# Three moves in the order of work: the product of gate sums on GpSimd, the search for gates on VectorE, one gate line on TensorE

## The chip, the cores and the metric

One Trainium2 chip, of which the kernel uses one core. The metric is the device time of one execution in microseconds, less is better. The engines are named as in the profile: PE is TensorE's matrix multiplication and PEld its weight loads, DVE is VectorE, ACT is ScalarE, POOL is GpSimd, SP is the engine that issues most DMAs.

## The reference

The computation is attention with pooled queries, followed by a layer that sends 128 of 576 tokens of each batch through a small network. All arrays are float32. B is 8, H is 8, S is 1152, D is 64.

```python
# attention
q_pool = q.reshape(B, H, S // 2, 2, D).mean(axis=3)
scores = np.matmul(q_pool, k.transpose(0, 1, 3, 2)) / np.sqrt(D)
attn = softmax(scores)                         # 576 x 1152 for each of 64 heads
x = heads_side_by_side(np.matmul(attn, v))     # (8, 576, 512)
# routing: 128 of 576 tokens in each batch
scores = np.einsum('bsd,d->bs', x, w_gate)
out = x.copy()
for b in range(B):
    top_idx = np.argpartition(-scores[b], 128)[:128]
    xe = x[b, top_idx]
    ye = np.maximum(xe @ w1, 0.0) @ w2         # 512 -> 1024 -> 512
    g = 1.0 / (1.0 + np.exp(-scores[b, top_idx]))
    out[b, top_idx] = x[b, top_idx] + g[:, None] * ye
```

## The kernel before

**Halves.** The work runs over 32 pairs of heads (8 batches, 4 pairs each), and each pair in two halves of 288 pooled queries, so 64 halves in all. The order of instructions on each engine is written out by hand; each engine takes its queue in that order and waits by semaphores. In the loop of `run` half number h issues, in this order: the scores of h (PE, L818, 36 matmuls in nine tiles of `ps`; after each tile ACT takes the exponent into `p`, L825); the places called "mid"; `gated` of half h-3; `folded` of h; the places called "sums"; `multiplied` of h-2; the values of h-1 (PE, L836, 36 matmuls, copied by ACT into `two`, L844, and added on POOL into `av`, L846); and at last the places called "end". The PSUM tile `ps` has four buffers, so a fifth tile waits until ACT has emptied the first.

**Around the exponents.** `folded` lets POOL add exponents (`acc`, L857, three additions in a half), and DVE add them up further (`fold`, L862; `sum`, L872). `drained` transposes `av` into `avb` (DVE, L915). `multiplied` multiplies `avb` with the weights of the gate (`prod`, POOL, L925). `gated` sums that up on DVE (`red`, L981), and in the second half of a pair it multiplies the sum with the reciprocal of the softmax's sums into `part` (L986: on POOL, and on DVE for the last two pairs of the last batch).

**Routing.** With the fourth pair of a batch the generator `routed` starts. It is cut into pieces by `yield`, and the value yielded says at which place of a half the next piece runs. Its steps: `line` (DVE, L1010) adds the four `part`. In batches 0 to 5 ACT copies it into 32 partitions and DVE adds the groups; in batch 6, the last but one, one matmul with `merge` does that (PE, L1024), and ACT copies its result into `total` (L1031). SP writes `total` to DRAM and reads it back spread over the partitions (`row`, `sc_row`, `gate_sc`, L1035 to L1038). DVE then ranks the tokens by comparisons (L1085 to L1104), and the ranks and gates go through DRAM into `lines`. Two searches over `lines` on DVE (both L1169, 128x640) find the token of each slot (`found_token`, from which `index` comes, L1178) and its gate (`own_gate`). POOL gathers the tokens with an indirect DMA (`xe`, L1188); PE transposes them (L1205), multiplies with `w1` (L1216) and `w2` (L1229); ACT multiplies with `own_gate` into `y` (L1248), POOL adds, and an indirect DMA scatters the result (L1254).

**The end.** After the last half `run` places the remaining pieces by hand: products with `w2` of batch 5 and 6 fill PE while the gate of the last batch is worked out in a chain over POOL, DVE, PE and ACT (`prod`, `red`, `part`, `line`, `diag`, L1046, and a matmul of it, L1056).

Of the kernel before, what the change touches and what calls it, by code (L numbers as in the profile page):

```python
# [10 lines left out]
P = 128  # L11
# [3 lines left out]
F32 = mybir.dt.float32  # L15
# [6 lines left out]
def _rows_of(ap_1d: bass.AP, parts: int) -> bass.AP:  # L22

    return dataclasses.replace(ap_1d, ap=[[0, parts]] + [list(x) for x in ap_1d.ap])
# [3 lines left out]
def _any_scores(  # L28
# [451 lines left out]
    in_pair = [(j, t) for j in range(2) for t in range(NF)] + [(0, NF)]  # L480
    upcoming = load_pair(*pairs[0])
    run(prepare_pair(upcoming))
    preparing = iter(())
    routing = iter(())
# [43 lines left out]
    for _ in range(2):  # L528
        advance(None)
        one, two = None, one  # L530
    run(routing)
    run(routed(B - 1, x))


class _Plain:
# [439 lines left out]
    def gated(self, half):  # L975

        nc, pair, hb = self.nc, half["pair"], self.HB
        if half["s"] == 0:
            pair["red"] = self.small.tile([P, self.QB], F32, name="red")
        ns = slice(half["s"] * hb, (half["s"] + 1) * hb)  # L980
        nc.vector.tensor_reduce(pair["red"][:, ns], pair["prod"][:, ns, :], AX.X, ALU.add)  # L981
        if half["s"] == 1:

            ending = pair["b"] == self.B - 1 and pair["hp"] >= self.NPAIR - 2
            engine = nc.vector if ending else nc.gpsimd
            engine.tensor_tensor(  # L986
                out=pair["part"][:, pair["hp"], :],
                in0=pair["red"][:, :],
                in1=pair["rec"][:, :],
                op=ALU.mult,  # L990
            )
            if pair["hp"] == self.NPAIR - 1:
                self.routing.append([pair["b"], self.routed(pair["b"], pair["part"]), "sums"])
# [6 lines left out]
    def routed(self, b, part):  # L1000


        nc, ffn, Sp, NT, NF = self.nc, self.ffn, self.Sp, self.NT, self.NF
        tiles = [(t, P if t < NF else self.TAIL) for t in range(NT)]
        mid = "mid" if b < self.B - 2 else True
# [7 lines left out]
        sc = ffn.tile([P, NT], F32, name="gate_sc")  # L1013
        if b < self.B - 1:

            yield "mid"
            if b < self.B - 2:
                groups = self.side_by_side(line)
                yield True
                total = self.added(groups)  # L1020
            else:
                total = self.small.tile([BLK, self.QB], F32, name="total")
                ps = self.banks()[:, 0, 0 : self.QB]
                nc.tensor.matmul(  # L1024
                    ps,
                    lhsT=self.merge.rearrange("p g j -> p (g j)"),
                    rhs=line[:, :],
                    start=True,
                    stop=True,
                )  # L1030
                nc.scalar.copy(total[:, :], ps[0:BLK, :])  # L1031
            sc_row = ffn.tile([P, NT * P], F32, name="sc_row")
            row = self.dram.tile([Sp], F32, name="row")
            nc.gpsimd.memset(sc[:, NF:], 0.0)
            nc.sync.dma_start(row.rearrange("(i n) -> i n", i=BLK), total[:, :])  # L1035
            nc.sync.dma_start(sc_row[:, 0:Sp], _rows_of(row[:], P))
            nc.sync.dma_start(sc[:, 0:NF], row[0 : NF * P].rearrange("(t p) -> p t", p=P))
            nc.sync.dma_start(  # L1038
                sc[0 : self.TAIL, NF:], row[NF * P :].rearrange("(t p) -> p t", p=self.TAIL)
            )  # L1040
            yield True
            yield True
        else:

            diag = ffn.tile([P, self.QB, BLK], F32, name="diag", bufs=1)
            nc.vector.tensor_tensor(  # L1046
                out=diag[:, :, :],
                in0=line[:, :].unsqueeze(2).broadcast_to([P, self.QB, BLK]),
                in1=self.same[:, :].unsqueeze(1).broadcast_to([P, self.QB, BLK]),
                op=ALU.mult,  # L1050
            )
            yield True
            sc_row = self.line_of_scores()
            ps = self.banks()
            for s in range(2):
                nc.tensor.matmul(  # L1056
                    ps[:, s, 0 : self.HALF],
                    lhsT=self.ones[:, :],
                    rhs=diag[:, s * self.HB : (s + 1) * self.HB, :].rearrange("p n i -> p (n i)"),
                    start=True,  # L1060
                    stop=True,
                )
            nc.scalar.copy(
                sc_row[:, 0:Sp].rearrange("p (i s n) -> p s n i", s=2, n=self.HB),
                ps[:, :, 0 : self.HALF].rearrange("p s (n i) -> p s n i", i=BLK),
            )
            yield True
            self.columns(sc, sc_row)
# [3 lines left out]
            out=gate[:, :], in0=sc[:, :], scalar1=-88.0, scalar2=None, op0=ALU.max  # L1072
# [7 lines left out]
        for t, rows in tiles:  # L1080
            at = t * P
            cmp = ffn.tile([P, Sp], F32, name="cmp", bufs=1)
            own = sc[0:rows, t : t + 1]
            if t > 0:
                nc.vector.tensor_scalar(  # L1085
                    out=cmp[0:rows, 0:at],
# [8 lines left out]
                out=cmp[0:rows, at:Sp],  # L1095
# [9 lines left out]
                out=tie[0:rows, 0:rows],  # L1105
# [16 lines left out]
            out=gate[:, :], in0=gate[:, :], scalar1=1.0, scalar2=None, op0=ALU.add  # L1122
# [5 lines left out]
        else:  # L1128
# [8 lines left out]
            lines = ffn.tile([P, P, 2, NT], F32, name="lines", bufs=1)  # L1137
            nc.sync.dma_start(lines.rearrange("p i a t -> p (i a t)"), _rows_of(row[:], P))

        for s0, w in self.slots:  # L1140
            pick = ffn.tile([P, NT, P], F32, name="pick", bufs=1)
            index = ffn.tile([P, 1], I32, name="index")
            own_gate = ffn.tile([P, 1], F32, name="own_gate")
            if b == self.B - 1:

                nc.vector.tensor_tensor(
                    out=pick[:, :, 0:w],
                    in0=self.slot_f[:, s0 : s0 + w].unsqueeze(1).broadcast_to([P, NT, w]),
                    in1=rank[:, :].unsqueeze(2).broadcast_to([P, NT, w]),
                    op=ALU.is_equal,  # L1150
                )
                yield True
                ps = self.banks()[:, 0, 0:2]
                for t, rows in tiles:
                    nc.tensor.matmul(  # L1155
                        ps[0:w, :],
                        lhsT=pick[0:rows, t, 0:w],
                        rhs=meta[0:rows, t, :],
                        start=(t == 0),
                        stop=(t == NT - 1),  # L1160
                    )
                nc.scalar.copy(index[0:w, :], ps[0:w, 0:1])
                nc.scalar.copy(own_gate[0:w, :], ps[0:w, 1:2])
            else:
                yield True

                found = self.small.tile([P, 1], F32, name="found_token")
                for of, to in ((self.token_line, found), (lines[:, :, 1, :], own_gate)):
                    nc.vector.scalar_tensor_tensor(  # L1169
                        out=pick.rearrange("p t i -> p (t i)").rearrange("p (i t) -> p i t", t=NT)[0:w],  # L1170
                        in0=lines[0:w, :, 0, :],
                        scalar=self.token[0:w, s0 // P : s0 // P + 1],
                        in1=of[0:w, :, :],
                        op0=ALU.is_equal,
                        op1=ALU.mult,
                        accum_out=to[0:w, :],
                    )
                nc.vector.tensor_scalar(  # L1178
                    out=index[0:w, :],
                    in0=found[0:w, :],  # L1180
                    scalar1=float(b * Sp),
                    scalar2=None,
                    op0=ALU.add,
                )

                yield "sums" if b < self.B - 2 else True
            xe = ffn.tile([P, self.Dm], F32, name="xe")
            nc.gpsimd.indirect_dma_start(  # L1188
                out=xe[0:w, :],
# [5 lines left out]
            )  # L1195
            yield True
            if b < self.B - 2:
                yield True
            if b != self.B - 2:
                yield mid  # L1200
# [36 lines left out]
            if b == self.B - 1:  # L1237
                nc.vector.scalar_tensor_tensor(
                    out=xe[0:w, :],
# [6 lines left out]
            else:  # L1246
# [8 lines left out]
                out=rows_out,  # L1255
# [65 lines left out]
    def run(self):  # L1321
        nc = self.nc
        pairs = [(b, hp) for b in range(self.B) for hp in range(self.NPAIR)]
        n_halves = 2 * len(pairs)
        halves = []
# [10 lines left out]
        for h in range(n_halves):  # L1336
            n, s = divmod(h, 2)
            if s == 0:
                pair = upcoming
# [12 lines left out]
            half = {"pair": pair, "s": s}  # L1352
            halves.append(half)
            self.scores(half)
            if h > 1:

                of = halves[h - 2 - s]["pair"]
# [5 lines left out]
            if h > 2:  # L1363
                self.gated(halves[h - 3])
            self.folded(half)
            self.units("sums")
            if h > 1:
                self.multiplied(halves[h - 2])
# [18 lines left out]
        def pieces(unit, n=None):  # L1387
            for i, _ in enumerate(unit):
                if i + 1 == n:
                    break  # L1390
# [8 lines left out]
        self.drained(halves[-1])  # L1399
        self.multiplied(halves[-2])  # L1400
        self.multiplied(halves[-1])
        self.gated(halves[-2])
        pieces(older, 1)
        self.normalized(halves[-1]["pair"])
        for half in (halves[-3], halves[-1]):
            self.divided(half["pair"])
            self.stored(half["pair"])
        self.gated(halves[-1])
        _, new, _ = self.routing.pop()

        pieces(new, 1)
# [76 lines left out]
```

## Time and profile before

| what | us |
|---|---|
| median of 4 runs | 703.91 (703.86 to 703.99) |
| the profiled execution's own time | 703.96 |
| its span, from the first to the last instruction | 702.2 |
| PE busy | 692.0 (99%) |
| PE weight loads busy | 515.1 (73%) |
| DVE busy | 478.6 (68%) |
| ACT busy | 445.4 (63%) |
| POOL busy | 491.7 (70%) |
| granted TensorE clock | 0.998 |

The profiled execution lies 0.05 us above the median; 1.76 us of its time lie outside the span. Busy time is what an engine's instructions cover; matmuls are pipelined, so their rows overlap a little, and a row's start tells more than its length. In the chain of waits each row starts where the row before it ends, so that its lengths add up to time on the path to the end; "x72" there counts 36 matmuls that are each made of two passes.

### The profile page before, as it was taken

To read this page: it belongs to the slowest core of one execution; us is meant where nothing else is said; L and a number is where in the kernel's file an instruction comes from. 1 tells how busy PE (TensorE), PEld (TensorE's weight loads), DVE (VectorE), ACT (ScalarE), POOL (GpSimd) and SP (SyncE) were. 2 spreads that over 40 slices of the span, in tenths; PEclk is the share of its full clock that TensorE was granted. 3 is DMA by queue.
4 is the path that set the end of the run, shared out by engine and by line. 5 is a ranking of instruction groups with operands and counts; after the bars stand their busy time and mean duration, and the time that the engine had idled before them with its cause. 6 is when DMAs were issued, how large, how long until landed. Compare 5 with 4: busy or idle time off the path is not lost.

```text
span 702.2 us, 23365 instructions
## 1 busy us (share of the span) xinstructions
PE 692.0 (99%) x9948; PEld 515.1 (73%) x9948; DVE 478.6 (68%) x770; ACT 445.4 (63%) x963; POOL 491.7 (70%) x475
## 2 busy tenths in 40 slices
PE   8999999999999999999999999999999999999996
PEld 6667899999756887568775787757877578676673
DVE  3866677788836887278863888548884588668740
ACT  6677778777647775477745777557775477747210
POOL 5788888779837796397954879548886479956620
PEclk9999999999999999999999999999999999999999
DMA  8888886858782396824956269652686528711300
GB/s 178 174 183 178 182 155 130 141 120 155 131 146 68 78 162 117 153 67 95 183 98 122 68 125 169 118 90 64 139 154 131 89 53 174 135 19 47 59 33 35
DMA packets 389490, 82.86 MB, mean 118 GB/s; under 512 B 376640, under 2 KB 376640, under 8 KB 389376
## 3 DMA queue, kind: packets, MB, share of 16 engines
q1 hardware_dynamic: 387872, 76.49, 57.3%
q0 software_dynamic: 1280, 4.20, 1.8%
q8 instruction: 80, 1.31, 0.8%
q10 hardware_dynamic: 224, 0.59, 0.3%
q14 instruction: 34, 0.28, 0.1%
HBM read 69.65 MB, written 11.59 MB: 116 GB/s over the span
## 4 chain that ended last, share of the span: by engine, by line
PE 96%; ACT 1%; DMA 1%; DVE 1%; POOL 0%; SPq 0%; issue 0%; POOLq 0%; DVEq 0%; ACTq 0%
PE ps L836 40%; PE ps L818 39%; PE ps L1216 8%; PE ps L1229 7%; DMA kb<-in_k_dram 1%; ACT p L825 1%; PE ps L1205 1%; SPq L759 0%; POOL prod L925 0%; DVE diag L1046 0%; PE ps L1155 0%; PE ps L1056 0%; ACT two L844 0%; PE ps L783 0%; POOL av L846 0%
## 5 line engine op out<-in xcount | busy, mean ns | idle before, releaser
L825 ACT ACTIVATE p<-ps 128x576 f32<-128x576 f32 x576 | 320.0, 697 | 1.0 <-PE ps L818 1.0
L836 PE MATMUL ps<-p,v_sb 64*64 64x288 f32 x4608 | 294.0, 403 | 0.0
L818 PE MATMUL ps<-qT,kT 64*64 64x288 f32 x4608 | 293.3, 403 | 0.0
L857 POOL TENSOR_TENSOR acc<-p 128x576 f32<-128x576 f32 x192 | 274.1, 1456 | 7.8 <-ACT p L825 7.7
L836 PEld LDWEIGHTS ps<-p,v_sb 64*64 64x64 f32 x4608 | 211.3, 133 | 69.5 <-ACT p L825 9.0
L818 PEld LDWEIGHTS ps<-qT,kT 64*64 64x64 f32 x4608 | 210.4, 133 | 69.2 <-ACT p L825 6.9
L862 DVE TRANSPOSE_TENSOR_REDUCE fold<-p 128x54 f32<-128x1728 f32 x64 | 126.0, 1969 | 56.9 <-ACT p L825 56.9
L862 DVE TRANSPOSE_TENSOR_REDUCE fold<-acc 128x54 f32<-128x1728 f32 x64 | 125.2, 1956 | 57.7 <-POOL acc L857 57.6
L844 ACT COPY two<-ps 128x576 f32<-128x576 f32 x64 | 40.9, 639 | 151.6 <-PE ps L836 148.2
L846 POOL TENSOR_TENSOR av<-two 128x288 f32<-128x288 f32 x64 | 51.2, 801 | 92.9 <-ACT two L844 82.5
L915 DVE STREAM_TRANSPOSE avb<-av 128x288 f32<-128x288 f32 x64 | 29.1, 454 | 67.2 <-POOL av L846 66.7
L1216 PEld LDWEIGHTS ps<-xeT,w 128*128 128x128 f32 x512 | 57.8, 192 | 2.7 <-ACT p L825 2.6
L1216 PE MATMUL ps<-xeT,w 128*128 128x128 f32 x512 | 59.3, 277 | 0.0
L1229 PE MATMUL ps<-w,hT 128*128 128x512 f32 x128 | 57.5, 599 | 0.0
L986 POOL TENSOR_TENSOR part<-red,rec 128x18 f32<-128x18 f32 x30 | 6.8, 226 | 64.3 <-DVE red L981 56.5
L925 POOL TENSOR_TENSOR prod<-avb,w_gate 128x288 f32<-128x288 f32 x64 | 51.6, 806 | 0.2
L732 POOL TENSOR_TENSOR qp<-qb 128x576 f32<-128x576 f32 x31 | 43.8, 1413 | 2.2 <-DMA qb<-in_q_dram 2.2
L1229 PEld LDWEIGHTS ps<-w,hT 128*128 128x128 f32 x128 | 23.5, 190 | 28.1 <-issue 25.8
L735 DVE STREAM_TRANSPOSE kT<-kb 128x1152 f32<-128x1152 f32 x31 | 42.0, 1355 | 0.0
L902 ACT ACTIVATE sums<-total,tiny 32x18 f32<-32x18 f32 x124 | 38.2, 308 | 2.9 <-DVE total L893 1.1
L959 POOL TENSOR_TENSOR x<-avb,rec 128x576 f32<-128x576 f32 x32 | 37.1, 1160 | 0.0
L1224 ACT ACTIVATE hT<-ps 128x512 f32<-128x512 f32 x16 | 9.6, 597 | 39.1 <-PE ps L1216 39.1
(96 smaller groups left out, 312.3 us busy)
## 6 DMA issues: line engine op xcount, KB each, us to landing
kb<-in_k_dram SPq DMA_DIRECT2D x124, 144.0 KB
qb<-in_q_dram SPq DMA_DIRECT2D x124, 144.0 KB
v_sb<-in_v_dram SPq DMA_DIRECT2D x124, 144.0 KB
out_dram<-x SPq DMA_DIRECT2D x128, 72.0 KB
lines<-row_rank SPq DMA_DIRECT2D x7, 640.0 KB
w<-in_moe_w_dram SPq DMA_DIRECT2D x8, 512.0 KB
sc_row<-row SPq DMA_DIRECT2D x7, 288.0 KB
acc<-in_q_dram ACTq DMA_DIRECT2D x2, 288.0 KB
```

The lines of the kernel that those rows point to most:

```text
L732: nc.gpsimd.tensor_tensor(out=qp[:, :, :], in0=pair["q"][:, :, 0, :], in1=pair["q"][:, :, 1, :], op=ALU.add)
L735: nc.vector.transpose(kT.rearrange("p (c g i) -> p c g i", c=self.NC, i=BLK), pair["k"].rearrange("p (g c) d -> p c g d", c=self.NC),)
L818: nc.tensor.matmul(sc[keys, j, 0:n], lhsT=pair["kT"][rows, c * P + keys.start : c * P + keys.stop], rhs=pair["qT"][rows, qs], start=True, ...
L825: nc.scalar.activation(p[:, c // G, c % G, :, :], sc[:, :, 0:n], AF.Exp, scale=self.scale)
L836: nc.tensor.matmul(av[j * self.D : (j + 1) * self.D, e, 0:n], lhsT=half["pair"]["v"][keys, j, c, :], rhs=half["p"][keys, c // G, c % G, j, :],
L844: nc.scalar.copy(two[:, :, :], av[:, :, 0:n])
L846: nc.gpsimd.tensor_tensor(out=half["av"][:, :], in0=two[:, 0, :], in1=two[:, 1, :], op=ALU.add)
L857: nc.gpsimd.tensor_tensor(out=acc[:, u, :], in0=units[:, 0, u, :], in1=units[:, 1, u, :], op=ALU.add)
L862: nc.vector.tensor_reduce(fold[:, a, :], of.rearrange("p u (m d) -> p (u m) d", d=BLK), AX.X, ALU.add, apply_transpose=True,)
L925: self.nc.gpsimd.tensor_tensor(out=pair["prod"][:, ns, :], in0=pair["avb"][:, ns, :], in1=self.w_gate[:, hp : hp + 1, :].broadcast_to([P, ...
L1216: nc.tensor.matmul(pv[:, f, 0:w], lhsT=self.w1[:, c, (f0 + f) * P : (f0 + f + 1) * P], rhs=xeT[:, c, 0:w], start=(c == 0), stop=(c == self ...
L1229: nc.tensor.matmul(ps[0:w, 0 : self.Dm], lhsT=hT[:, f, 0:w], rhs=self.w2[:, f, :], start=(f == 0), stop=(f == self.NFC - 1),)
```

## The change

Three moves. No instruction is added or removed, and none changes its size.

1. `gated` is split. The product into `part` becomes a function `scored` of its own, and `run` calls it behind `folded`, so that POOL has `part` behind the three additions of exponents and not ahead of them, in all 30 products on POOL. At the end the DVE product of the last pair but one stands behind the last transpose into `avb`, where it stood ahead of it.
2. In batches 0 to 5 the search for `own_gate` runs in the "end" of the half after the one in which the token is searched; `index` follows the first search at once. In batch 6 both stay in the same half, and `index` is computed between them.
3. In batch 6 the matmul of the gate line (L1024) and the copy into `total` move from the "mid" of a half to its "end": on PE from ahead of the transposes of batch 5 (L1205) and the values (L836) to behind them, ahead of the next scores; on ACT from ahead of the copies of L1208 and L844 to behind them, ahead of the next nine exponents. A `yield` further on is left out in this batch, so that the comparisons keep their half.

The order of SP's queue stays as it was. The cut diff:

```diff
@@ def gated
         nc.vector.tensor_reduce(pair["red"][:, ns], pair["prod"][:, ns, :], AX.X, ALU.add)
+
+    def scored(self, half):
+        nc, pair = self.nc, half["pair"]
         if half["s"] == 1:
             ending = pair["b"] == self.B - 1 and pair["hp"] >= self.NPAIR - 2
             engine = nc.vector if ending else nc.gpsimd
...
@@ def routed
-            yield "mid"
+            yield mid
             if b < self.B - 2:
                 groups = self.side_by_side(line)
                 yield True
                 total = self.added(groups)
             else:
+                yield True
                 total = self.small.tile([BLK, self.QB], F32, name="total")
...
             yield True
-            yield True
+            if b < self.B - 2:
+                yield True
...
-                found = self.small.tile([P, 1], F32, name="found_token")
-                for of, to in ((self.token_line, found), (lines[:, :, 1, :], own_gate)):
+                def search(of, to):
+                    at = ffn.tile([P, NT, P], F32, name="pick", bufs=1)
                     nc.vector.scalar_tensor_tensor(
...
+                found = self.small.tile([P, 1], F32, name="found_token")
+                search(self.token_line, found)
                 nc.vector.tensor_scalar(
...
+                if b == self.B - 2:
+                    search(lines[:, :, 1, :], own_gate)
                 yield "sums" if b < self.B - 2 else True
...
             if b < self.B - 2:
+                search(lines[:, :, 1, :], own_gate)
                 yield True
@@ def run
             if h > 2:
                 self.gated(halves[h - 3])
             self.folded(half)
+            if h > 2:
+                self.scored(halves[h - 3])
             self.units("sums")
...
         self.multiplied(halves[-1])
+        self.scored(halves[-3])
         self.gated(halves[-2])
...
         self.gated(halves[-1])
+        self.scored(halves[-1])
```

More of the change, by code (lines that the diff above doesn't have):

```diff
@@ L1140, in routed @@
         for s0, w in self.slots:
-            pick = ffn.tile([P, NT, P], F32, name="pick", bufs=1)
             index = ffn.tile([P, 1], I32, name="index")
@@ L1144, in routed @@
             if b == self.B - 1:
+                pick = ffn.tile([P, NT, P], F32, name="pick", bufs=1)
                 nc.vector.tensor_tensor(
@@ L1165, in routed @@
                 yield True
-                found = self.small.tile([P, 1], F32, name="found_token")
-                for of, to in ((self.token_line, found), (lines[:, :, 1, :], own_gate)):
+                def search(of, to):
+                    at = ffn.tile([P, NT, P], F32, name="pick", bufs=1)
                     nc.vector.scalar_tensor_tensor(
-                        out=pick.rearrange("p t i -> p (t i)").rearrange("p (i t) -> p i t", t=NT)[0:w],
+                        out=at.rearrange("p t i -> p (t i)").rearrange("p (i t) -> p i t", t=NT)[0:w],
                         in0=lines[0:w, :, 0, :],
```

## Prediction

> **What bounds the kernel now.** I read the page's busy times and the chain that ended last first.
>
> ```profile
> PE 692.0 (99%) x9948; PEld 515.1 (73%) x9948; DVE 478.6 (68%) x770; ACT 445.4 (63%) x963; POOL 491.7 (70%) x475
> PE 96%; ACT 1%; DMA 1%; DVE 1%; POOL 0%; SPq 0%; issue 0%; POOLq 0%; DVEq 0%; ACTq 0%
> ```
>
> PE carries the chain. The other engines stand still for a third of the time, so an earlier step on POOL or DVE is worth something only where PE waits for it. Of the waits, POOL's largest for `part` is this one (us, times, longest):
>
> ```profile
> POOL part L986 <- DVE red L981: 56.5, 28, 4.9
> ```
>
> With its two other releasers (4.6 and 3.2 us) POOL stands 64.3 us ahead of `part`. But this is idle time of an engine that is off the chain. So I looked for places where PE itself is late. The chain in order of time (start, length, what) repeats 4.37 us for the scores and 4.37 to 4.41 us for the values of a half, nearly without exception. Here is batch 5, with nothing but the transposes between them:
>
> ```profile
> 512.43 4.37 PE ps L818 x72
> 516.80 0.59 PE ps L1205 x4
> 517.39 4.53 PE ps L836 x72
> 521.91 4.37 PE ps L818 x72
> ```
>
> and here is the same place of batch 6, where the gate line stands:
>
> ```profile
> 597.90 0.47 ACT two L844
> 598.44 5.01 ACT p L825 x9
> 603.45 0.35 PE ps L1024 x2
> 603.80 0.48 PE ps L1205 x4
> 604.28 4.53 PE ps L836 x72
> 608.80 4.37 PE ps L818 x72
> ```
>
> From the start of the scores to the start of the values it takes 517.39 - 512.43 = 4.96 us in batch 5. In batch 6 the values before end at 597.83 (593.45 + 4.38 in the same view), and it takes 604.28 - 597.83 = 6.45 us. The 1.49 us between them are the price of the gate line where it stands: 1.25 us of waiting, and the matmul. The timeline says what it waits for (start, length, engine, line):
>
> ```profile
> 603.03 0.26 DVE L1010 TENSOR_REDUCE line<-part 128x18 f32<-128x72 f32 x1
> 603.43 0.37 PE L1024 MATMUL ps<-line,merge 128*128 128x18 f32 x2 [1.25 <-ACT p L825]
> ```
>
> The row names an exponent. The ninth exponent ends only at 603.44, while the matmul's operand `line` is done at 603.29 and its first weights load at 603.40: I take `line` to be the releaser. If it is an exponent that frees a tile of `ps`, the sum stays the same, as the changed place has neither wait.
>
> **Part 3, the gate line, is the only part that I expect on the path.** Removed: 1.49 us, as L1205 then follows the scores directly as in batch 5. Added: the same matmul between values and scores. `line` is then needed at about 597.83 + 4.96 + 4.53 = 607.3 and was ready at 603.29, so no wait. The tile it takes needs the exponent two places further on than the one L1205 needs, long done by then. What remains is its own pitch and the passage between 64x64 and 128x128 tiles. Own pitch: from L1024 to L1205 it is 603.65 - 603.43 = 0.22 us; the similar matmul at the end (L938, 36 columns) is followed after 0.14 us. Passage: four transposes take 0.59 us behind scores and 0.44 us among 128x128 tiles, so 0.15 going in; values take 4.53 us behind them and 4.37 behind scores, so 0.16 coming out. Sum 0.14 to 0.22 + 0.31 = 0.45 to 0.53; I take 0.45, as the pitch of 0.22 contains some of the way in. Bounds: 0.14 with no passage at all, and 0.75 (0.59 + 0.16) if it costs as much as the transposes. Net: -1.49 + 0.45 = -1.04 us, between -1.35 and -0.74.
>
> Here a rule speaks against this part. TensorEngine Tiling (Array Packing), Key Properties, says that changing the tiling mode drains TensorE. The rows above show such a cost (0.15 and 0.16 us), and before, L1024 shared one pair of passages with L1205, while it now has its own. Without the rule the sum would be -1.49 + 0.22 = -1.27 us, with it -1.04 us.
>
> Behind L1024 in PE's queue are the next scores; on ACT the copy into `total` (0.17 us) now stands behind `two` and ahead of nine exponents, which all wait for it. That cover is in the trace: in the half at 633.8 us ACT has the gate's exponential (0.21 us) in just this place, and the chain still gives 4.37 us for scores and for values. SP's issue of `row` is at 609.23 although `total` was done at 605.07, because four stores stand ahead of it. `total` will now be done at about 608.1, so SP is hardly later; the last read is issued at 612.3, and the comparisons start at 627.4 in their unchanged half. If that cover were gone, PE would lose what the landing exceeds 627.4 by.
>
> **Part 1, `part` behind the additions.** 30 products of 0.23 us change places with 30 x 3 additions of 1.46 us. Queued behind `part` are now `prod` and `av`, ahead of them less waiting than before: `av` waits for ACT's `two` anyway (82.5 us over the run). Who waits for `part`: only `line`, once in a batch, on DVE behind a fold that waits for the same additions; it comes at most 0.23 us behind them. POOL begins the additions up to 4.9 us earlier, DVE gets its fold earlier, and PE takes no note: 0. If POOL were the bound, the 64.3 us would be the gain; the chain puts POOL at 0%.
>
> **Part 2, the search.** One search of 1.91 us (the first takes 1.12) and its readout of 0.08 move by a half, in six batches, 12 us of DVE in all; `index` comes 2.0 us earlier. The half with both is the crowded one (DVE busy 8.71 of 8.75 us at 589.08 to 597.83). `own_gate` is needed by `y`, some 45 us after (505.5 against 549.6 in batch 5). The gather stands behind the additions on POOL and is issued at 506.95 with a median of 4.2 us to landing, for transposes at 516.73: early before, no later after. On PE: 0. The cover is DVE's slack to the exponents' buffers: the fold of `acc` ends at 602.7, and its `p` is written again at 609.5, 6.8 us later, against 2.0 us moved. Without cover it would be 6 x 2.0 = 12 us.
>
> **The end.** There the chain leaves PE for 6 us, and part 1 changes DVE's order:
>
> ```profile
> 656.51 0.79 POOL L846 TENSOR_TENSOR av<-two 128x288 f32<-128x288 f32 x1 [1.15 <-ACT two L844]
> 656.72 0.61 DVE L986 TENSOR_TENSOR part<-red,rec 128x18 f32<-128x18 f32 x1
> 657.26 1.54 POOL L925 TENSOR_TENSOR prod<-avb,w_gate 128x288 f32<-128x288 f32 x2
> 657.33 0.48 DVE L915 STREAM_TRANSPOSE avb<-av 128x288 f32<-128x288 f32 x1
> 658.08 0.46 DVE L981 TENSOR_REDUCE red<-prod 128x9 f32<-128x288 f32 x1 [0.28 <-POOL prod L925]
> 658.84 0.45 DVE L981 TENSOR_REDUCE red<-prod 128x9 f32<-128x288 f32 x1
> 659.32 0.63 DVE L986 TENSOR_TENSOR part<-red,rec 128x18 f32<-128x18 f32 x1
> 660.30 1.35 DVE L1046 TENSOR_TENSOR diag<-line,same 128x576 f32<-128x576 f32 x1
> 661.80 1.21 PE L1056 MATMUL ps<-diag,ones 128*128 128x288 f32 x4
> ```
>
> The two `part` on DVE end 0.03 us behind a POOL instruction (657.33 against 657.30; 659.95 against 659.90, as the second POOL row of 1.13 us began at 658.77), 0.6 us for what POOL does in 0.23. The first moves behind L915, to about 657.8, into the first product, which ends at 658.05; the reduction that follows began at 658.08. So +0.03 us if DVE gets in between the two products as it did at 657.30. If not, it ends at 658.84, the reductions and the reciprocal follow to 659.95, the second `part` waits for the second product of L959 until 661.06, and `diag` (0.62 us once POOL is done at 661.03) ends at 662.03 where it ended at 661.65: +0.38. An earlier end gains no more than 0.1, since PE's transposes end at 661.70. I take +0.03, the row in the same place.
>
> The page SBUF — State Buffer, Who interferes with whom, makes that an exclusive lock: a DVE instruction with two inputs in SBUF and a reading GpSimd instruction exclude each other for a whole instruction, and issue order decides. It agrees with the ends of the rows, and would make +0.03 or +0.38 as the second product issues behind or ahead of DVE.
>
> **Sum.** -1.04 + 0.03 = -1.01 us on the profiled 703.96, 702.95; on the median, 0.05 lower, 702.90. Changes within 0.2% (1.41 us, about what a measurement of this kernel can tell from no change: 702.50 to 705.32) count as the same.
>
> **Rivals.** *Everything gained (0.15):* L1024 costs 0.14 without passage, and the freed POOL also takes away what the values lose in the six rows of 4.41 us (6 x 0.04 = 0.24): 703.91 - 1.49 + 0.14 - 0.24 = 702.32, faster. For it: weight loads of L836 wait 9.0 us for exponents in 43 places. Against: PE's rows hardly show it, and POOL is not what they wait for. *The end pays (0.15):* DVE loses its place between the products: 702.87 + 0.38 = 703.25, the same by the bound. *The change brings nothing (0.06):* the matmul waits in its new place for its tile as long as it did: 703.91. Against: the exponents are done 4 us before. *Slower (0.07):* POOL's additions, up to 4.9 us earlier, now run beside ACT's exponents and slow them. The ninth score tile of a half and the values' tile are already waited for by 0.2 us (35 and 43 weight loads), so PE loses as soon as nine exponents take over some 5.3 us in place of 5.00; 0.2 us in 28 halves are 5.6: 703.91 - 1.04 + 5.6 = 708.5. Against: they take 5.00 us in halves where additions run beside them (598.44 and 625.69) as in others. The forecast keeps 0.57.
>
> The range takes in the bound of the cheap matmul less the small waits (702.3, rounded up to 702.4 with the chance beyond it) and -0.74 with +0.38 (703.55): 702.4 to 703.6. Faster by over 0.2%: 0.15 and a little of the forecast's lower edge, 0.16; the same 0.77; slower 0.07.
>
> **What would show it.** Right: in batch 6 the chain goes scores, L1205 with 0.59, values 4.53, the gate matmul with 0.2 to 0.35, scores, all on PE; POOL's wait of 56.5 us for `red` is gone and stands at `av`, its busy time unchanged; L1056 starts 1.0 us earlier than before, within 0.1. Wrong: a wait on PE ahead of the gate matmul, scores of 4.6 us and more behind it, nine exponents over 5.1 us, or L1056 earlier by 0.7 us or less.

## The result, and the profile after

The changed kernel takes 704.86 us (median of 35 runs, 704.09 to 706.51), the kernel before 703.99 us beside it (55 runs, 703.6 to 705.89). The ratio is 1.0011, interval 1.0007 to 1.0016: slower by 0.8 us (the medians differ by 0.87), where 1.0 us less was predicted. By the bound of 0.2% that is no change, but it lies outside the predicted range. The profiled execution took 704.37 us, its span is 702.63 us.

Most of what the prediction listed as its proof is in the trace. First the page of the kernel after, busy times and the chain by engine:

```profile
PE 693.6 (99%) x9948; PEld 497.1 (71%) x9948; DVE 497.5 (71%) x770; ACT 446.0 (63%) x963; POOL 492.1 (70%) x475
PE 97%; DMA 1%; DVE 1%; POOL 0%; SPq 0%; issue 0%; ACT 0%; POOLq 0%; DVEq 0%; ACTq 0%
```

ACT's 1% of the chain, the wait for the gate line, is gone. PE, still the whole chain, is busy 1.6 us longer (693.6 against 692.0) with the same instructions. The waits (us, times, longest) show the first move as it was read from the code: POOL's 56.5 us for `red` have shrunk to 9.7 and stand elsewhere.

```profile
POOL av L846 <- ACT two L844: 116.9, 28, 8.8
POOL acc L857 <- ACT p L825: 36.5, 41, 1.9
PEld ps L818 <- ACT p L825: 15.3, 63, 0.4
POOL part L990 <- DVE red L981: 9.7, 10, 1.4
```

The third row was not foreseen: weight loads of the scores wait for exponents 63 times and 15.3 us, before 35 times and 6.9 us. Now the place of the gate line in batch 6, in the chain in order of time (start, length, what):

```profile
599.17 4.37 PE ps L818 x72
603.54 0.59 PE ps L1217 x4
604.12 4.53 PE ps L836 x72
608.65 0.33 PE ps L1029 x2
608.98 4.53 PE ps L818 x72
```

That is the predicted order, all on PE. From one start of scores to the next it takes 9.91 us here, 1.14 us less than before. The gate matmul costs 0.33 us of its own and 0.16 us of passage into the scores behind it (4.53 in place of 4.37). So the gain that was predicted did come. The loss stands elsewhere, in a half of the next kind (this one in batch 1):

```profile
247.44 4.67 PE ps L818 x72
252.11 4.42 PE ps L836 x72
256.53 4.37 PE ps L818 x72
```

Before, the same half took:

```profile
247.57 4.36 PE ps L818 x72
251.93 4.37 PE ps L836 x72
```

Scores of 4.67 us and values of 4.42 us stand where 4.36 and 4.37 were. There are six such halves, one in each of batches 0 to 5. By the distances from one start of scores to the next they are 0.18, 0.43, 0.41, 0.31, 0.31 and 0.34 us longer than the same halves before: 1.98 us in all. The halves around them take back 0.29 us, the end adds 0.07 us. With -1.14 us at the gate line that makes +0.62 us; from the second half's scores to the end of the span the kernel took 680.68 us, 0.64 us more than before (680.04). So the sign that the prediction hung on the whole sum failed: the first matmul of `diag` starts at 662.14 us in the chain in place of 661.81, 0.33 us later, where 1.0 us earlier was forecast.

What these six halves have in common is the gather of `xe`. Here is the timeline of the same stretch (start, length, engine, line, operation, idle time and what ended it):

```profile
247.53 0.64 ACT L844 COPY two<-ps 128x576 f32<-128x576 f32 x1 [1.91 <-POOL acc L857]
247.63 1.14 POOL L1199 DMA_INDIRECT xe<-out_dram,index  x1
248.07 0.66 ACT L825 ACTIVATE p<-ps 128x576 f32<-128x576 f32 x1
249.06 1.74 ACT L825 ACTIVATE p<-ps 128x576 f32<-128x576 f32 x3 [0.34 <-PE ps L818]
249.76 0.21 PEld L818 LDWEIGHTS ps<-qT,kT 64*64 64x64 f32 x8 [0.41 <-ACT p L825]
```

The second exponent of the half begins 0.99 us behind the first, where 0.54 us is usual, and ACT idles for 0.34 us of it, waiting for PE; 0.7 us later PE waits for an exponent, as `ps` has four buffers. But PE was not late: its matmuls still started every 0.485 us for a tile. Late is what PE reports. Here are the trace's records of PE's semaphore, which the exponents wait for, and the starts of the exponents, all counted from the start of the gather on POOL. Without a pause a report comes every 0.485 us.

```
                 gather at   reports of PE            exponents start
before, batch 1    250.84    0.14             1.38    0.02  0.55  1.08  1.61
before, batch 2    336.19    0.16  0.73       1.50    0.04  0.58  1.11  1.64
after, batch 1     247.63    0.31  1.41 1.51  1.77    0.44        1.44  1.98
after, batch 2     333.35    0.33  1.41 1.51  1.78    0.46        1.44  1.98
```

After, the second tile's report is due at 0.80 and comes at 1.41; the third's, due at 1.28, comes 0.1 us behind it; the fourth is on time. ACT would have taken the second tile at 0.98. Before, the pause is there too, and behind each gather and scatter of the loop: in this profile and the one before no report is recorded from 0.74 to 1.29 us behind their start. (Where a record is missing, as at 0.62 in batch 1 before, the exponent of 1.08 shows that the report itself had come.) But it costs nothing. The gather stands 3.5 us behind the first matmul of the scores, in the middle of these nine exponents without a gap:

```profile
248.20 5.00 ACT L825 ACTIVATE p<-ps 128x576 f32<-128x576 f32 x9
250.84 1.14 POOL L1188 DMA_INDIRECT xe<-out_dram,index  x1 [0.16 <-issue]
```

A report is due at 0.62, just ahead of the pause, and the next, due at 1.11, is wanted only at 1.61: ACT takes 0.53 us for a tile and PE 0.485 us, so ACT's distance has grown from 0.13 us at the first tile to about 0.5 us at the ninth. The change has moved the gather to 0.4 us behind the first matmul (in batch 0 to 0.4 us ahead of it). There the distance is 0.13 to 0.2 us, and a report is due in the middle of the pause.

### The profile page after: what moved, and what is told of

Its sections match the earlier page's. It is cut to its first block, busy times and chain, and to the rows that moved or that the text cites. A ratio compares the mean times of both kernels' runs of the same rounds, so it can differ in the third digit from the quotient of the medians.

```text
span 702.6 us, 23364 instructions
## 1 busy us (share of the span) xinstructions
PE 693.6 (99%) x9948; PEld 497.1 (71%) x9948; DVE 497.5 (71%) x770; ACT 446.0 (63%) x963; POOL 492.1 (70%) x475
## 3 DMA queue, kind: packets, MB, share of 16 engines
q8 instruction: 80, 1.31, 0.8%
## 4 chain that ended last, share of the span: by engine, by line
PE 97%; DMA 1%; DVE 1%; POOL 0%; SPq 0%; issue 0%; ACT 0%; POOLq 0%; DVEq 0%; ACTq 0%
PE ps L836 40%; PE ps L818 40%; PE ps L1228 8%; PE ps L1241 7%; DMA kb<-in_k_dram 1%; PE ps L1217 1%; SPq L759 0%; POOL prod L925 0%; DVE diag L1052 0%; PE ps L1161 0%; PE ps L1062 0%; PE ps L783 0%; POOL av L846 0%; DVE xe L1250 0%; POOL out_dram L1266 0%
## 5 line engine op out<-in xcount | busy, mean ns | idle before, releaser
L836 PE MATMUL ps<-p,v_sb 64*64 64x288 f32 x4608 | 293.9, 404 | 0.0
L836 PEld LDWEIGHTS ps<-p,v_sb 64*64 64x64 f32 x4608 | 204.3, 133 | 76.8 <-ACT p L825 10.5
L818 PEld LDWEIGHTS ps<-qT,kT 64*64 64x64 f32 x4608 | 199.4, 133 | 81.2 <-ACT p L825 15.3
L844 ACT COPY two<-ps 128x576 f32<-128x576 f32 x64 | 40.9, 639 | 151.3 <-PE ps L836 130.9
L1110 DVE SCALAR_TENSOR_TENSOR tie<-sc_row,gate_sc,before 128x128 f32<-128x128 f32 (+1 forms) x40 | 45.9, 1147 | 0.0
```

Of the source, the lines that this page charges most:

```text
L818: nc.tensor.matmul(sc[keys, j, 0:n], lhsT=pair["kT"][rows, c * P + keys.start : c * P + keys.stop], rhs=pair["qT"][rows, qs], start=True, ...
L836: nc.tensor.matmul(av[j * self.D : (j + 1) * self.D, e, 0:n], lhsT=half["pair"]["v"][keys, j, c, :], rhs=half["p"][keys, c // G, c % G, j, :],
L1110: nc.vector.scalar_tensor_tensor(out=tie[0:rows, 0:rows], in0=sc_row[0:rows, at : at + rows], scalar=own, in1=self.before[0:rows, 0:rows], ...
```

## The experiments

The theories, before any of these runs: the gather's pause, moved to the start of the scores (A); POOL's additions beside ACT slow the exponents (B); the moved search makes DVE late (C); the gate line costs in its new place what it saves (D). After the first group A became A2, in which the pause belongs to the execution and not to the kernel, with E beside it, in which the third move makes the loss.

The runs were made in three groups on three chips: chip 8 (the first four), chip 5 (the next four) and chip 11 (the last four), each with the kernel before beside it (704.32, 704.14 and 704.24 us). One thing must be known to read their spans: the loading at the start varies. The second half's scores began between 21.95 and 23.62 us in these profiles, without regard to the kernel, so the medians hold a scatter of up to 1.7 us that is none of the change's. The table gives the span from there to the end ("body"), which leaves it out. The body in turn holds what follows the issue of the last scatter, and this varies too: 4.3 us before, 4.6 us in two of the runs, 3.9 us with the plain load. So the last two columns, which lie ahead of it, tell more than a small difference between bodies. "Gather" is where the gather is issued, in us behind the first matmul of the scores (batches 1 to 5; batch 0 differs), "six" and "gate" are what the six halves and the gate half take longer than before, and "pause" says whether that profile shows PE's reports held back behind gathers.

| kernel | chip | ratio (interval) | body | gather | pause | six | gate |
|---|---|---|---|---|---|---|---|
| before | - | 1 | 680.04 | 3.5 | yes | 0 | 0 |
| changed | - | 1.0011 (1.0007 to 1.0016) | 680.68 | 0.4 | yes | 1.98 | -1.14 |
| gate line only | 8 | 0.9987 (0.9976 to 0.9999) | 679.30 | 3.5 | no | 0 | -1.07 |
| products only | 8 | 0.9978 (0.9968 to 0.9988) | 678.90 | 1.3 | no | 0 | -1.21 |
| search only | 8 | 1.0007 (0.9987 to 1.0028) | 680.08 | 2.9 | no | 0 | -0.11 |
| products and search | 8 | 0.9972 (0.9961 to 0.9984) | 678.94 | 0.4 | no | 0 | -1.21 |
| changed, again | 5 | 1.0003 (0.9994 to 1.0012) | 680.73 | 0.4 | yes | 2.12 | -1.14 |
| changed, gather behind `av` | 5 | 0.9987 (0.9978 to 0.9997) | 679.23 | 2.0 | yes | 0.24 | -1.07 |
| products and search, again | 5 | 1.0005 (0.9996 to 1.0014) | 680.20 | 0.4 | yes | 1.62 | -1.24 |
| changed, plain load | 5 | 0.998 (0.997 to 0.999) | 678.56 | none | no | 0 | -1.08 |
| products and search, gather behind `av` | 11 | 0.9984 (0.9975 to 0.9992) | 679.16 | 2.0 | no | 0 | -1.21 |
| products only, again | 11 | 0.9984 (0.9974 to 0.9993) | 678.87 | 1.3 | no | 0 | -1.21 |
| changed, gather behind `prod` | 11 | 0.9981 (0.9968 to 0.9994) | 679.03 | 1.2 | no | 0 | -1.08 |
| changed, a third time | 11 | 0.999 (0.9981 to 0.9999) | 679.10 | 0.4 | no | 0 | -1.08 |

### The moves one by one

**Gate line only**: of the change only the third move.

```diff
-            yield "mid"
+            yield mid
...
             else:
+                yield True
...
-            yield True
+            if b < self.B - 2:
+                yield True
```

> The kernel before with the third move alone (gate line of batch 6 behind the values). Theory A (while GpSimd works on an indirect gather no semaphore is updated on any engine for about 0.6 us, and the change brings the gathers of batches 0 to 5 into the first score tiles of a half, where ACT has caught up with PE and needs each update): the gather stays where it was, so no half of scores is long, and the gate line brings what the sum said, 1.0 us: ratio to before 0.9986. Theory B (GpSimd's additions, now earlier, run beside the exponents and slow them) and theory C (the moved search makes DVE late) say the same here. Theory D (the gate line itself costs in its new place what it saved): ratio 1.000.

Measured: 703.57 us, body 0.74 us less than before, of which the gate half has -1.07 us (4.53 us of values, 0.33 of the gate matmul, 4.53 of scores); what follows the issue of the last scatter took 0.28 us more. The term of the prediction was right.

**Products only**: the first move, `scored` behind `folded`, and nothing else.

> The kernel before with the first move alone (products of gate sums behind the additions). The additions end about 3 us earlier, but the index of the gather still comes behind both searches, so the gather can't start before about 2.4 us into the scores, and its pause falls where ACT is already three tiles behind PE. Theory A: no loss, ratio 1.000 (within 0.0004), each half of scores 4.37 us. Theory B: the whole loss, six halves of 4.55 to 4.7 us, ratio 1.0022 to 1.0027 (1.5 to 1.9 us). Theory C: 1.000.

Measured: 703.06 us. This was expected by no theory. The chain at the gate line, which stands in its old place in this kernel:

```profile
593.42 4.37 PE ps L836 x72
597.79 4.37 PE ps L818 x72
602.15 0.33 PE ps L1028 x2
602.48 0.56 PE ps L1209 x4
603.04 4.58 PE ps L836 x72
607.62 4.37 PE ps L818 x72
```

The wait of 1.25 us is gone although the matmul has not moved. `line` starts on DVE at 599.22 us where it started at 603.03 (here its length in ns, then its start in us):

```profile
L1014 DVE TENSOR_REDUCE line<-part x1: 274/274/274, 599.2 to 599.2; 128x18 f32<-128x72 f32 x1
```

The reason is in the queues: POOL, no longer held by `part`, adds the exponents earlier, DVE folds them earlier, and `line`, which stands behind a fold in DVE's queue, comes 3.8 us earlier. The first and the third move take away the same wait, and the first does it better (-1.21 against -1.07 us), as the matmul shares one passage with the transposes.

**Search only**: the second move alone.

```diff
-                for of, to in ((self.token_line, found), (lines[:, :, 1, :], own_gate)):
+                search(self.token_line, found)
...
             if b < self.B - 2:
+                search(lines[:, :, 1, :], own_gate)
                 yield True
```

> The kernel before with the second move alone (search for gates a half later). The index comes 2 us earlier, but the gather stands behind additions that still wait for the reductions, and starts about 2.5 us into the scores. Theory A: no loss, ratio 1.000. Theory B: 1.000. Theory C: the whole loss, ratio 1.0022 to 1.0027.

Measured: 705.38 us with a wide interval; this profile's start was a late one (23.38 us). Its body is that of before within 0.04 us: the gate half is 0.11 us shorter, what follows the issue of the last scatter 0.15 us longer. The move alone brings the gather only from 3.5 to 2.9 us, as POOL still reaches it late.

**Products and search**: both, without the third move.

> The first and the second move together, without the gate line. Theory A: only together do they free the gather, which starts some 0.4 us into the scores; the loss of five or six halves, 1.5 to 1.9 us, and no gain: ratio 1.0022 to 1.0027, scores of 4.55 to 4.7 us in the halves with a gather, and the second exponent there late by 0.2 to 0.35 us. Theory B: as its part in the run with the first move alone, and no more. Theory C: as its part in the run with the second move alone.

Measured: 702.84 us, the fastest of the group, with the gather at 0.4 us as in the changed kernel. The same stretch as above:

```profile
247.50 4.37 PE ps L818 x72
251.87 4.37 PE ps L836 x72
256.23 4.37 PE ps L818 x72
```

No long half, and PE's semaphore reports at 247.52, 248.00, 248.49, 248.97, 249.46, without a pause. So an early gather is not enough for a loss, and of the theories named so far none stood: exponents and DVE's lateness (B and C) show in no row, the gate line (D) gains, and the pause (A) was missing. But it was missing in all four profiles of this chip, also where it costs nothing. That left two: the pause belongs to the execution (A2), or the third move makes it (E).

### The pause, with and without an early gather

The next group ran on chip 5. **Changed, again** is the kernel of the change; **products and search, again** is that of the run before.

> The changed kernel once more, beside its neighbours. The run of the first and second move together had its gathers where the changed kernel has them, 0.4 us into the scores, and yet no late semaphore and no long half of scores, while the profiles of before and of the change both show semaphores of PE late by 0.5 to 0.7 us behind a gather or a scatter. Theory A2: the pause belongs to the execution or the chip and not to the kernel; where it is absent the changed kernel takes the same as the first and second move together plus one more passage between tile sizes for the gate line (0.2 to 0.5 us): ratio 0.9975 to 0.9985 to the kernel before; where it is present, five halves of scores of 4.55 to 4.7 us and a ratio of 1.001. Theory E: the third move makes the loss, in whatever way: long halves of scores here again, ratio 1.001, while the two moves alone stay at 0.997.

> The first and second move without the third, once more. Theory A2: with the pause five halves of scores of 4.55 to 4.7 us, a loss of 1.5 to 1.9 us against a gain of 1.05 us, ratio 1.0005 to 1.0012; without it 0.997 to 0.9985 as before, 0.2 to 0.5 us below the changed kernel. Theory E: 0.997 to 0.9985 in both cases, and 1.5 us or more below the changed kernel.

Measured: 704.55 and 704.75 us. On this chip products and search has five halves longer by 0.29 to 0.35 us, and that of batch 0 by 0.09 us. Batch 1:

```profile
247.55 4.54 PE ps L818 x71
252.09 4.42 PE ps L836 x72
256.51 4.37 PE ps L818 x72
```

and the two reports due at 0.83 and 1.31 us behind the gather's start come at 1.31 and 1.41 us. One kernel, 678.94 us of body without the pause and 680.20 with it. The third move is not the cause. The kernel's other runs fit this: on chip 8 nine of twelve took 702.96 us or less, on chip 5 none of eleven took less than 703.98.

**Changed, gather behind `av`**: the gather of batches 0 to 5 goes to the "end" of its half, 1.6 us later, and all else stays.

```diff
-                yield "sums" if b < self.B - 2 else True
+                yield True
             xe = ffn.tile([P, self.Dm], F32, name="xe")
             nc.gpsimd.indirect_dma_start(
...
-            yield True
             if b < self.B - 2:
                 search(lines[:, :, 1, :], own_gate)
-                yield True
+            yield True
```

> The changed kernel with the gathers of batches 0 to 5 moved behind prod and av on GpSimd, about 2.8 us later in the half, where they nearly stood before the change. Theory A2: no long half of scores on any chip; ratio 0.9975 to 0.9985, faster than the changed kernel by 1.5 to 1.9 us where that one shows the pause, and equal to it where it does not. Theory E: the ratio of the changed kernel, as the third move is still there.

Measured: 703.48 us, ratio 0.9987. The pause is still behind every gather, but only one half is longer, by 0.24 us. The half shown above, from its chain and its timeline:

```profile
247.58 4.36 PE ps L818 x72
251.95 4.37 PE ps L836 x72
```

```profile
248.21 5.00 ACT L825 ACTIVATE p<-ps 128x576 f32<-128x576 f32 x9
249.35 1.14 POOL L1199 DMA_INDIRECT xe<-out_dram,index  x1 [0.16 <-issue]
```

Why it costs so little, again counted from the start of the gather:

```
            gather at   reports of PE             exponents start
batch 1       249.35    0.19        1.37  1.64    0.47  1.00  1.53  2.06
batch 4       505.49    0.19  1.28  1.38  1.64    0.46  1.30  1.85  2.38
```

A report is due at 0.67 here. In the other five batches it still came in time, and no exponent there was late by more than 0.07 us; in batch 4 it fell into the pause and the exponent waited until 1.30. The next, due at 1.16, is wanted at 1.53, behind the pause. So I read it that the place among the reports decides as much as ACT's distance, and that this place is on the edge.

**Changed, plain load**: in batches 0 to 5 SP loads 128 fixed rows of the batch in place of the gather, so the tokens are not the chosen ones.

```diff
+            if b < self.B - 2:
+                nc.sync.dma_start(xe[0:w, :], rows_out[b * Sp : b * Sp + w, :])
+            else:
                 nc.gpsimd.indirect_dma_start(
```

> The changed kernel without the indirect gathers of batches 0 to 5: SP loads 128 fixed rows of each batch in their place, so that the chosen tokens' rows are left out and the network works on others. Theory A2: without a gather no late semaphore in those halves and no long half of scores, ratio 0.997 to 0.9985 on any chip. Theory E: the ratio of the changed kernel.

Measured: 702.58 us, no long half (scores of 4.37 us at 247.44, values of 4.37 behind them). The six halves had neither the gather nor a pause, while the pause behind the scatters remained in the same profile, 3.7 us into the scores, where it costs nothing. So without the indirect transfer the loss is gone, on the chip where it was seen. That a plain load in the same place would be harmless isn't shown: SP issued these loads 6.3 to 8.5 us behind the first matmul, not at 0.4. Its body holds 0.5 us more of gain at the very end, behind the last scatter, which I don't put down to the gather.

### On a third chip

**Products and search, gather behind `av`** joins two edits shown above, **products only, again** repeats the first move alone, **changed, gather behind `prod`** puts the gather 0.8 us later than the change does, and **changed, a third time** is the change.

> The first two moves without the third, and the gather of batches 0 to 5 issued 2 us later (behind the additions of av). Theory A2 (a pause of the semaphores with each indirect gather costs 0.25 to 0.35 us in each of six halves where it falls on the first two tiles, the first move alone takes the wait at the gate line away): ratio 0.997 to 0.9985 whether the profile shows late semaphore updates or not. Rival F (the first two moves differ between chips for another reason than the place of the gather): 1.0000 to 1.001 where the profile shows late updates.

> The first move alone, with the gather 1.3 us into the scores. Theory A2: where the profile shows late updates, the pause falls 0.8 us later than in the changed kernel, on the third and fourth tile, when the exponents are about one tile behind TensorE: none or small losses, ratio 0.9975 to 0.999. If the ratio is 1.0000 or more with late updates, an offset of 1.3 us is still too early.

```diff
-                yield "sums" if b < self.B - 2 else True
+                yield "prod" if b < self.B - 2 else True
```

(with a place "prod" in `run`, behind `multiplied`)

> The changed kernel with the gather of batches 0 to 5 behind the first product of gate sums, some 0.8 us later than in the change. Theory A2: where the profile shows late updates, between the changed kernel and the one with the gather behind av: ratio 0.9985 to 1.0003 and rows of scores in the six halves of 4.4 to 4.55 us. Without late updates 0.998 to 0.999.

> The changed kernel itself on the same chip, to tell whether the pause is there. Theory A2: six scores of 4.55 us and more and ratio 1.0003 to 1.0015 with late updates in the profile, or 0.997 to 0.9985 without.

Measured: 703.35, 703.01, 703.18 and 704.35 us. The pause was absent from this chip's profiles. (The first kernel has two gaps of 0.97 us, where the report due at 0.67 us has no record; but the next, due at 1.16 us, is on time, and no exponent is late.) So what a gather at 1.2 or 1.3 us would lose to it was not measured, and the rival F of the first expectation was not decided by these runs. What came of it is the change without its loss. The chain of the changed kernel here:

```profile
249.01 4.37 PE ps L818 x72
253.37 4.37 PE ps L836 x72
...
599.26 4.36 PE ps L818 x72
603.62 0.59 PE ps L1217 x4
604.21 4.53 PE ps L836 x72
608.73 0.33 PE ps L1029 x2
609.06 4.53 PE ps L818 x72
```

Its body is 679.10 us, 0.94 us less than before. Its profiled execution still took 704.46 us, since its start was 1.4 us late; five of its twelve runs took 703.0 to 703.3 us, the others 704.3 us and more.

The first move alone was faster than the kernel before on both chips it ran on (0.9978 and 0.9984). Against the changed kernel it ran beside only on chip 11, with a body 0.23 us shorter (678.87 against 679.10). Neither of its profiles held the pause, so its gather at 1.3 us is not proven safe. Where the pause was seen, the gather behind `av` lost 0.24 us in all.

## Why the prediction was wrong

**The sum's main term was right.** -1.04 us at the gate line was predicted, -1.07 us was measured for the move alone in its half. The gate matmul's place cost 0.33 + 0.16 = 0.49 us, predicted 0.45. The rule weighed there (the Trainium skill, TensorEngine Tiling (Array Packing), Key Properties: a change of the tiling mode drains TensorE) fits: the scores behind the matmul take 4.53 us in place of 4.37.

**The end was right.** From the last `av` to the matmul of `diag` it takes 662.14 - 656.84 = 5.30 us after and 661.81 - 656.51 = 5.30 us before, where 0.03 us was taken and 0.38 us kept as a bound. The first `part` on DVE now stands beside a product at no cost to the chain.

**The step that failed is part 2's "early before, no later after ... On PE: 0".** It asked of the gather only when it lands, and not what its issue does to others. And it let `index` come 2.0 us earlier while POOL reached the gather when it did before, although part 1 frees POOL: with additions that end at 247.48 in place of 250.68 us, both moves together bring it 3.1 us forward, into the first tiles of the scores. There it costs 1.98 us in the profile, in place of 0. The runs show this by the place (0.24 us with the gather at 2.0 us, on the chip where the change lost 2.12), by the execution (0 without the pause, with the gather at 0.4 us) and, less strictly, by the transfer (0 without the gather, as the plain load stood elsewhere).

**Part 1's "PE takes no note: 0" was off too,** in the other direction. Its own working had "DVE gets its fold earlier", and `line` "behind a fold that waits for the same additions"; carried on to the wait at the gate line it would have led to what products only measured, -1.21 us. The prediction had priced the wait under part 3 and did not ask whether another part removed it first. Given part 1, part 3 gains nothing: its gate half is 0.13 us longer (-1.08 against -1.21 us). So where the pause was absent the changed kernel came near the forecast (a body 0.94 us shorter on chip 11, against the -1.01 of the sum), but by luck: part 1 alone, priced at 0, brought 1.17 us there.

**The rivals.** "Slower" had the sign, and saw that PE loses when exponents come late. Its mechanism was wrong: exponents beside POOL's additions take 5.00 us for nine with the additions early (products only and gather behind `av`), and in the long halves only the second starts late. "Everything gained" needed a passage that costs nothing, and 0.16 us stood in every profile. "The change brings nothing" and "the end pays" were not seen.

**What stays open** is what makes the pause present. On chip 5 it stood in the profiles of all three kernels with the gather, on chips 8 and 11 in none. The changed kernel's runs beside the result never fell below 704.09 us, while chip 11 has them at 703.0. Whether it is the chip, the place of buffers or queues, or something else of an execution, was not tried. The chip of the result itself is not on record.

## What to carry to other kernels

A step off the critical path, moved earlier, takes its side effects along: look where its DMA issue lands among the instructions of the engine on the path, not only whether its data comes in time. When several parts of a change free the same queue, work out their places together, and price each wait once: the part that makes its releaser early may take the wait that another part is credited with. Where such an issue disturbs a handover between two engines, move it by half a step and see whether the loss goes.

## What the runs showed of the hardware

Behind an indirect DMA issued from GpSimd, in some executions, PE's semaphore reports were held back from about 0.75 to 1.3 us (at most 1.6) after its start and, where two were due, then came within about 0.1 us of each other, while the matmuls went on in their pitch of 0.485 us a tile. In the half shown no engine's semaphore has a record between 248.48 and 249.04 us. Such a gap alone says little, as gaps of 0.5 us stand in profiles without the pause too. A count says more: from 0.85 to 1.2 us behind the eleven gathers and scatters of the loop, the profiles with the pause hold no record of PE's semaphore and 0 to 5 of those that other DMAs update, the profiles without it 5 to 11 and 14 to 65. So it isn't PE's reports alone; but ACT's report some 1.09 us behind each scatter is there in both. Around the loads of as many rows from SP PE's reports kept their pitch. In other executions of the same instructions the reports came on time, and the same kernel was 1.3 us faster in its body (678.94 against 680.20). I had not expected an engine off the chain to delay semaphores between others, nor that this would differ from one execution to the next.
